# A batch-normed convolution on one Trainium2 core: one weight sum moved from GpSimd to VectorE, and one weight load split into eight transfers

## The chip, the core and the metric

The kernel runs on one core of a Trainium2 chip. The metric is the device time of one execution in microseconds (us). Engines are named as the profile names them: PE is TensorE (PEld its weight load), DVE is VectorE, ACT is ScalarE, POOL is GpSimd and SP is SyncE, which here only issues transfers. PSUM is the memory in which PE leaves its sums; it has eight banks here.

## The reference: what is computed

```python
B, S, C = 2, 2048, 1024          # x: (B, S, C), w: (3, C, C), all bfloat16
xp = jnp.pad(x, ((0, 0), (1, 1), (0, 0)))
y = sum(jnp.einsum('bsc,cd->bsd', xp[:, k:k + S, :], w[k]) for k in range(3))
inv_std = 1.0 / jnp.sqrt(var + 1e-5)
y = (y - mean) * (g * inv_std) + b
return silu(y)
```

It is a convolution of width 3 along the sequence, from 1024 to 1024 channels, with a scale and a shift for each output channel and silu behind it.

## The kernel before

**The method.** The convolution is computed in a transformed domain: six neighbouring outputs come from eight products instead of eighteen. The input is transformed once by small matmuls with a constant matrix (line 231), whose results are copied out of PSUM to `T_sb` (lines 249 and 251). The three taps of the weights become eight: tap 0 and tap 2 as they are (points j = 0 and j = 7), and three pairs (j = 1 to 6) made from a sum of taps 0 and 2, the "even sum" `e0`, `e1`, `e2` (w0 + w2, w0 + 4 w2, 4 w0 + w2), plus and minus tap 1 (for the first pair) or twice tap 1 (for the other two). The pairs are called `u`; line 150 makes each half of a pair by one instruction on POOL.

**The work.** Output channels are cut into eight blocks of 128 (`dc`), the batch has two entries (`bi`); a unit is one block for one entry, and there are sixteen, in the order (0,0), (0,1), (1,0), (1,1) and so on. A product is eight matmuls of 128x128 by 342 columns over the eight channel tiles, for one point j (line 279). A unit uses four banks, and units alternate between banks 0 to 3 and 4 to 7. Between the products ACT copies banks out (lines 288 and 290) and DVE combines them (line 294); in the end ACT applies silu (line 298) and SP stores (line 371).

**The order of PE** is written out by hand. The first unit is mixed with the input transforms (`ORDER`). In `run`, a unit's products are (bank, j) = (3,1), (0,3), (3,2), (0,4), (2,5), (2,6), with `early` (only the second unit) moving (2,5) ahead of (0,4). The last two products of a unit, j = 0 and j = 7, come during the unit behind it: `rest` gives them, and the list `also` says behind which step (`behind(1)` to `behind(6)`) they and other pieces are issued. For the second unit they are issued in the third unit, j = 0 behind step 4 and j = 7 behind step 5 (line 578). They add to banks that DVE has combined before: j = 0 to the unit's bank 0, which the combine of line 361 writes, and j = 7 to bank 3, which that of line 363 writes.

**The weights of the second block** (dc = 1) are prepared by the four pieces of `prepare_second` (line 183): the first pair on POOL; then the sum of the second (ACT scales tap 2 by 4, POOL adds); then ACT doubles tap 1 and POOL makes the second pair; and last `fourth`: ACT scales tap 0 by 4 (line 127), POOL adds tap 2 (line 137), POOL makes the third pair (line 150). `third` is issued behind step 1 of the second unit and `fourth` behind step 4 (line 576). Later blocks use `even_vector` (line 139) for their second and third sum: one DVE instruction that multiplies and adds (line 143).

**The loads** are issued by SP in the order of lines 522 to 537: input tiles `xw` of the first entry with the weights of block 0 between them, then the first two halves of the second entry, `xl` (the 48 rows left over at the end of the second entry, in three transfers of 15, 26 and 7 rows, line 534), seven more tiles, and the weights of block 1 as one transfer of 128 rows of 6 KB (line 537). A tile of the second entry reuses the place of a tile that PE has read.

Of the kernel before, what the change touches and what calls it, by code (L numbers as in the profile page):

```python
# [13 lines left out]
P = 128  # L14
# [4 lines left out]
LROWS = 48  # L19
SROW = 66  # L20
# [16 lines left out]
def kernel(  # L37
# [9 lines left out]
    nc = tc.nc  # L47
# [40 lines left out]
    xt, raw = {}, {}  # L88


    small = xlpool.tile([P, CT * P], BF16, name="xl")
    nc.vector.memset(small, 0.0)

    def load_small(bi, cuts=()):
        cuts = (0, *cuts, LROWS)
        for lo, hi in zip(cuts, cuts[1:]):
            nc.sync.dma_start(out=small[bi * SROW + lo:bi * SROW + hi], in_=xl[bi, lo:hi])

    def load_x(bi, ct, parts=1, second=nc.scalar):
        t = xpool.tile([P, NF, P], BF16, name="xw")  # L100
        xt[bi, ct] = t
        step = NF // parts
        for q in range(parts):
            s = slice(q * step, (q + 1) * step)
            (second if q else nc.sync).dma_start(out=t[:, s], in_=x[bi, ct, :, s])

    def load_w(dc, taps):
        if dc not in raw:
            raw[dc] = wpools[dc // 2 % 2].tile([P, 3, CT, P], BF16, name=f"wch{dc // 2 % 2}")
        if len(taps) == 3:  # L110
            nc.sync.dma_start(out=raw[dc], in_=w[dc])
        else:
            for k in taps:
                nc.sync.dma_start(out=raw[dc][:, k], in_=w[dc, :, k])
# [5 lines left out]
    def idle(work):  # L120
        if work:
            work.pop(0)()

    def scaled(src, by, eng):
        t = spool.tile([P, CT, P], BF16, name="w1x2")
        if eng is nc.scalar:
            nc.scalar.mul(t, src, by)
        else:
            eng.tensor_scalar(t, src, by, 0.0, op0=ALU.mult, op1=ALU.add)
        return t  # L130

    def double_w(dc, eng):
        double[dc] = scaled(raw[dc][:, 1], 2.0, eng)

    def even(dc, q, a, b):
        sums[dc, q] = epool.tile([P, CT, P], FP32, name=f"e{q}")
        nc.gpsimd.tensor_tensor(sums[dc, q], a, b, op=ALU.add)  # L137

    def even_vector(dc, q):
        w0, w2 = raw[dc][:, 0], raw[dc][:, 2]  # L140
        sums[dc, q] = e = epool.tile([P, CT, P], FP32, name=f"e{q}")
        f, h = (w2, w0) if q == 1 else (w0, w2)
        nc.vector.scalar_tensor_tensor(out=e, in0=f, scalar=4.0, in1=h, op0=ALU.mult, op1=ALU.add)  # L143

    def transform_w(dc, q, signs=(0, 1)):
        o = double[dc] if q else raw[dc][:, 1]
        if (dc, q) not in wts:
            wts[dc, q] = upool.tile([P, 2, CT, P], BF16, name=f"u{q}")
        for i in signs:
            nc.gpsimd.tensor_tensor(wts[dc, q][:, i], sums[dc, q], o, op=(ALU.add, ALU.subtract)[i])  # L150
# [32 lines left out]
    def prepare_second(dc):  # L183
        w0, w2 = raw[dc][:, 0], raw[dc][:, 2]

        def first():
            even(dc, 0, w0, w2)
            transform_w(dc, 0)

        def second():  # L190
            even(dc, 1, scaled(w2, 4.0, nc.scalar), w0)

        def third():
            double_w(dc, nc.scalar)
            transform_w(dc, 1)

        def fourth():
            even(dc, 2, scaled(w0, 4.0, nc.scalar), w2)
            transform_w(dc, 2)

        return first, second, third, fourth
# [321 lines left out]
    load_x(0, 1, 2)  # L523
    nc.sync.dma_start(out=prm, in_=prm_in)
    load_small(0)
    scales()
    nc.scalar.activation(dummy[:, 1:2], dummy[:, 0:1], ACT.Silu)
    for ct in range(2, CT):
        load_x(0, ct)
        if ct == 2:  # L530
            load_w(0, (0, 2))
    load_w(0, (1,))
    load_x(1, 0, 2, nc.sync)
    load_small(1, (15, 41))
    for ct in range(1, CT):
        load_x(1, ct)
    load_w(1, (0, 1, 2))

# [3 lines left out]
    second = list(prepare_second(1))  # L544
# [27 lines left out]
    for i, (dc, bi) in enumerate(seq[1:-1], 1):  # L572
        unit = Unit(dc, bi, i % 2 * 4)
        also = prev.rest(quiet)
        if i == 1:
            also = [(1, second[0]), (4, second[1])] + also
        if i == 2:
            also = prev.rest(quiet, 5, 4)
        if i == 3:
            also = also + [(1, lambda: idle(act_work)), (1, lambda: idle(dve_work))]  # L580
        if i == len(seq) - 2:
            also = prev.rest(quiet, 4, 5)
        unit.run(
            quiet, also,
            2 if i == 2 else dc + 2 if bi == 1 and 0 < dc < DC - 2 else None, i == 2, i == 1, i == 3,
        )
        if bi == 0 and dc + 3 < DC:
            load_w(dc + 3, (0, 1, 2))
        prev.store(nc.sync)
        prev = unit  # L590

    dc, bi = seq[-1]
# [80 lines left out]
```

## Time and profile before

| | us |
|---|---|
| three runs | 181.49, 181.79, 181.71 |
| median | 181.71 |
| the profiled execution | 181.6 |
| its span, first to last instruction | 179.8 |
| PE busy in the span | 173.3 |
| DVE busy | 148.2 |
| POOL busy | 140.6 |
| ACT busy | 110.8 |

The times of all rows of the profile are microseconds from the start of the span. A line of a timeline gives start, length, engine, line of the kernel, operation, what is written and read, and how many instructions were merged (x2); in brackets is the idle time ahead of it and what ended that. A line of the waits gives who waited for whom, the sum, how many times, and the longest. The chain that ended last is PE for 88% of the span. The clock granted to PE was 0.999 of full speed.

### The profile page before, as it was taken

To read this page: it belongs to the slowest core of one execution; us is meant where nothing else is said; L and a number is where in the kernel's file an instruction comes from. 1 tells how busy PE (TensorE), PEld (TensorE's weight loads), DVE (VectorE), ACT (ScalarE), POOL (GpSimd) and SP (SyncE) were. 2 spreads that over 40 slices of the span, in tenths; PEclk is the share of its full clock that TensorE was granted. 3 is DMA by queue.
4 is the path that set the end of the run, shared out by engine and by line. 5 is a ranking of instruction groups with operands and counts; after the bars stand their busy time and mean duration, and the time that the engine had idled before them with its cause. 6 is when DMAs were issued, how large, how long until landed. Compare 5 with 4: busy or idle time off the path is not lost.

```text
span 179.8 us, 3491 instructions
## 1 busy us (share of the span) xinstructions
PE 173.3 (96%) x1372; PEld 124.4 (69%) x1372; DVE 148.2 (82%) x193; ACT 110.8 (62%) x175; POOL 140.6 (78%) x77
## 2 busy tenths in 40 slices
PE   7889999999999999999999999999999999999991
PEld 5768888766666666666666666666666666668891
DVE  1568788987969999998898989898998997766792
ACT  3779989968364747365545654555456454573774
POOL 2499999999997979999999999999979978000000
PEclk9999999999999999999999999999999999999999
DMA  5999993170325030823073306430303020213033
GB/s 161 373 415 380 401 417 132 51 303 4 131 79 231 0 131 0 225 86 131 0 177 133 131 0 127 183 131 2 128 7 131 0 112 25 87 44 128 8 142 121
DMA packets 7507, 24.58 MB, mean 137 GB/s; under 512 B 1123, under 2 KB 1635, under 8 KB 7491
## 3 DMA queue, kind: packets, MB, share of 16 engines
q1 hardware_dynamic: 6915, 23.74, 36.1%
q10 hardware_dynamic: 576, 0.63, 1.0%
q8 instruction: 10, 0.16, 0.4%
q14 instruction: 6, 0.05, 0.1%
HBM read 14.93 MB, written 9.44 MB: 136 GB/s over the span
## 4 chain that ended last, share of the span: by engine, by line
PE 88%; DMA 5%; DVE 3%; ACT 1%; issue 0%; ACTq 0%; DVEq 0%
PE ps L279 75%; PE ps L231 8%; DMA xw<-in_x_dram 5%; PE ps L398 5%; DVE ps L294 2%; DVE t L294 1%; ACT yh L298 1%; ACT T_sb L249 1%; ACTq L78 0%; DVEq L662 0%; DVE sd L294 0%; PE ps L240 0%; PE ps L596 0%; DVEq L294 0%
## 5 line engine op out<-in xcount | busy, mean ns | idle before, releaser
L279 PE MATMUL ps<-T_sb,u 128*128 128x342 bf16 (+2 forms) x768 | 109.4, 298 | 0.0
L279 PEld LDWEIGHTS <-u 128*128 128x128 bf16 x768 | 72.2, 97 | 32.8 <-POOL u L150 0.3
L150 POOL TENSOR_TENSOR u<-e,w1x 128x1024 bf16<-128x1024 f32 x32 | 71.5, 2259 | 5.6 <-DVE e L143 5.5
L279 PE MATMUL ps<-T_sb,wch 128*128 128x342 bf16 (+2 forms) x256 | 39.5, 299 | 0.4 <-DVE ps L294 0.4
L294 DVE SCALAR_TENSOR_TENSOR t<-ps,sd 128x684 f32<-128x684 f32 (+2 forms) x49 | 37.6, 819 | 0.6
L298 ACT ACTIVATE yT<-ps,beta,scale 128x342 bf16<-128x342 f32 (+1 forms) x42 | 29.1, 727 | 12.6 <-PE ps L279 12.6
L150 POOL TENSOR_TENSOR u<-e,wch 128x1024 bf16<-128x1024 f32 x16 | 35.7, 2247 | 0.5
L279 PEld LDWEIGHTS <-wch 128*128 128x128 bf16 x256 | 24.2, 97 | 11.1 <-issue 0.5
L288 ACT COPY pc<-ps 128x342 f32<-128x342 f32 (+2 forms) x32 | 13.6, 424 | 28.4 <-PE ps L279 25.7
L249 ACT CAST T_sb<-ps 128x1008 bf16<-128x1008 f32 (+1 forms) x32 | 27.3, 879 | 3.9 <-PE ps L231 3.5
L251 DVE CAST T_sb<-ps 128x1008 bf16<-128x1008 f32 (+2 forms) x18 | 19.3, 1094 | 9.7 <-PE ps L231 9.2
L294 DVE SCALAR_TENSOR_TENSOR ps<-ps,t 128x684 f32<-128x684 f32 (+2 forms) x32 | 26.5, 829 | 0.7
L294 DVE SCALAR_TENSOR_TENSOR ps<-ps,pc 128x342 f32<-128x342 f32 (+2 forms) x34 | 16.9, 497 | 12.1 <-PE ps L279 8.8
L231 PE MATMUL ps<-rm,xw 128*128 128x168 bf16 x256 | 23.4, 239 | 1.6 <-DMA xw<-in_x_dram 1.4
L143 DVE SCALAR_TENSOR_TENSOR e<-wch 128x1024 f32<-128x1024 bf16 x12 | 24.6, 2052 | 0.0
L231 PEld LDWEIGHTS <-xw 128*128 128x128 bf16 x256 | 19.9, 99 | 4.8 <-DMA xw<-in_x_dram 2.4
L137 POOL TENSOR_TENSOR e<-wch 128x1024 f32<-128x1024 bf16 x8 | 19.0, 2372 | 0.1
L298 ACT ACTIVATE yT<-t,beta,scale 128x684 bf16<-128x684 f32 x15 | 14.4, 958 | 0.0
L294 DVE SCALAR_TENSOR_TENSOR t<-ps,t 128x684 f32<-128x684 f32 (+2 forms) x17 | 13.9, 817 | 0.0
L288 ACT COPY sd<-ps 128x342 f32<-128x342 f32 (+2 forms) x16 | 6.8, 426 | 10.3 <-PE ps L279 9.3
L290 ACT ACTIVATE pc<-ps 128x342 f32<-128x342 f32 (+2 forms) x16 | 7.0, 438 | 8.8 <-PE ps L279 6.1
L294 DVE SCALAR_TENSOR_TENSOR sd<-pc,ps 128x342 f32<-128x342 f32 (+2 forms) x17 | 8.2, 484 | 4.1 <-ACT sd L288 4.0
(45 smaller groups left out, 67.3 us busy)
## 6 DMA issues: line engine op xcount, KB each, us to landing
out_dram<-yT SPq DMA_DIRECT2D x15, 576.0 KB, 2.8
xw<-in_x_dram SPq DMA_DIRECT2D x13, 512.0 KB, 6.4
wch<-in_w_dram SPq DMA_DIRECT2D x7, 768.0 KB, 5.5
xw<-in_x_dram SPq DMA_DIRECT2D x4, 256.0 KB, 8.4
wch<-in_w_dram SPq DMA_DIRECT2D x3, 256.0 KB, 5.2
xw<-in_x_dram ACTq DMA_DIRECT2D x2, 256.0 KB, 4.6
out_dram<-yh SPq DMA_DIRECT2D x1, 256.0 KB, 2.0
out_dram<-yh SPq DMA_DIRECT2D x1, 128.0 KB
```

The costliest lines, as they stand in the source:

```text
L137: nc.gpsimd.tensor_tensor(sums[dc, q], a, b, op=ALU.add)
L143: nc.vector.scalar_tensor_tensor(out=e, in0=f, scalar=4.0, in1=h, op0=ALU.mult, op1=ALU.add)
L150: nc.gpsimd.tensor_tensor(wts[dc, q][:, i], sums[dc, q], o, op=(ALU.add, ALU.subtract)[i])
L231: nc.tensor.matmul(src[:, q // per, q % per], lhsT=xt[bi, ct][:, f + q], rhs=rm, start=True, stop=True)
L249: nc.scalar.copy(dst, src)
L251: nc.vector.tensor_copy(dst, src)
L279: nc.tensor.matmul(self.bank[q], lhsT=lhsT, rhs=T_sb[self.bi][:, ct, j, nsl], start=not add and ct == 0, stop=ct == CT - 1, skip_group_che ...
L288: nc.scalar.copy(dst, self.bank[q])
L290: nc.scalar.mul(dst, self.bank[q], by)
L294: nc.vector.scalar_tensor_tensor(out=out, in0=in0, scalar=scalar, in1=in1, op0=ALU.mult, op1=op1)
L298: nc.scalar.activation(self.yT[:, rows, self.y0:self.y0 + self.hi - self.lo], src, ACT.Silu, bias=beta[:, dc:dc + 1], scale=scale[:, dc:dc ...
L398: nc.tensor.matmul(self.bank[q], lhsT=lhsT, rhs=T_sb[self.bi][:, ct, j, :], start=not add and ct == 0, stop=ct == CT - 1, skip_group_check ...
```

## The change

The even sum of the second block's third pair is made by DVE (`even_vector`), in one instruction from the loaded taps, instead of by ACT and POOL. The piece `fourth`, with the two POOL instructions of the pair, is issued behind step 3 of the second unit instead of step 4; there it stands behind the combine of line 341 and ahead of that of line 348. The left-over rows of the second entry come in one transfer instead of three, and the weights of block 1 in eight, of 96, 1, 2, 3, 4, 5, 6 and 11 rows, instead of one. `load_w` and `load_small` change accordingly. PE's order stays as it is.

```diff
-    def load_small(bi, cuts=()):
-        cuts = (0, *cuts, LROWS)
-        for lo, hi in zip(cuts, cuts[1:]):
-            nc.sync.dma_start(out=small[bi * SROW + lo:bi * SROW + hi], in_=xl[bi, lo:hi])
+    def load_small(bi):
+        nc.sync.dma_start(out=small[bi * SROW:bi * SROW + LROWS], in_=xl[bi])
...
-    def load_w(dc, taps):
+    def load_w(dc, taps, cuts=()):
         if dc not in raw:
             raw[dc] = wpools[dc // 2 % 2].tile([P, 3, CT, P], BF16, name=f"wch{dc // 2 % 2}")
         if len(taps) == 3:
-            nc.sync.dma_start(out=raw[dc], in_=w[dc])
+            cuts = (0, *cuts, P)
+            for lo, hi in zip(cuts, cuts[1:]):
+                nc.sync.dma_start(out=raw[dc][lo:hi], in_=w[dc, lo:hi])
...
         def fourth():
-            even(dc, 2, scaled(w0, 4.0, nc.scalar), w2)
+            even_vector(dc, 2)
             transform_w(dc, 2)
...
-    load_small(1, (15, 41))
+    load_small(1)
     for ct in range(1, CT):
         load_x(1, ct)
-    load_w(1, (0, 1, 2))
+    load_w(1, (0, 1, 2), (96, 97, 99, 102, 106, 111, 117))
...
         if i == 1:
-            also = [(1, second[0]), (4, second[1])] + also
+            also = [(1, second[0]), (3, second[1])] + also
```

## The prediction

> **What bounds the kernel now.** I began with the page's busy shares, then the list of waits, then the timelines of TensorE (PE), GpSimd (POOL) and VectorE (DVE) one by one around the second and third unit, and last SyncE's queue. The page:
>
> ```profile
> PE 173.3 (96%) x1372; PEld 124.4 (69%) x1372; DVE 148.2 (82%) x193; ACT 110.8 (62%) x175; POOL 140.6 (78%) x77
> ```
>
> PE is the bound. Its matmuls follow each other without a gap from 14.2 us to 171 us, apart from one place; the first 10.8 us are the wait for the first inputs, the last 9 us are the drain of the last half unit. So the change is worth what it does to PE's gaps, and the waits have two rows for PE in its main stretch:
>
> ```profile
> PE ps L279 <- DVE ps L294: 0.4, 1, 0.4
> PEld L279 <- POOL u L150: 0.3, 1, 0.3
> ```
>
> The first is at 175.99, in the drain, which the change does not reach. The second is the place that it does reach. PE's and its weight loader's timelines:
>
> ```profile
> 47.79 1.32 PE L279 MATMUL ps<-T_sb,wch 128*128 128x342 bf16 x8
> 49.09 1.34 PE L279 MATMUL ps<-T_sb,u 128*128 128x342 bf16 x8
> ...
> 49.09 0.99 PEld L279 LDWEIGHTS <-u 128*128 128x128 bf16 x8 [0.33 <-POOL u L150]
> ```
>
> Matmuls of this shape start every 0.145 us, so eight from 47.79 would end with a start at 48.95; the next group starts at 49.09. PE loses 0.15 us there, waiting for the first product of the second block's third pair of transformed weights (u). POOL's timeline shows why:
>
> ```profile
> 40.51 4.24 POOL L150 TENSOR_TENSOR u<-e,w1x 128x1024 bf16<-128x1024 f32 x2
> 44.69 2.14 POOL L137 TENSOR_TENSOR e<-w1x,wch 128x1024 f32<-128x1024 bf16 x1
> 46.91 4.23 POOL L150 TENSOR_TENSOR u<-e,w1x 128x1024 bf16<-128x1024 f32 x2
> ```
>
> The row at 44.69 is the even sum that the change moves. POOL is busy without a gap up to 57.5, so taking 2.14 us from it brings the next pair forward.
>
> **The change, part by part.** (1) Gone: that sum on POOL, and on ScalarE (ACT) the scaling at 41.36 (1.06 us). ACT is not late for anyone here, and its three activations up to 44.96 come a microsecond earlier; its next copy (44.87) waits for PE anyway by 44.5. Value 0 for PE.
>
> (2) New on DVE: one sum of 128x1024, behind the second unit's first sd combine (40.50) and ahead of the combine at 42.18:
>
> ```profile
> 40.50 0.50 DVE L294 SCALAR_TENSOR_TENSOR sd<-pc,ps 128x342 f32<-128x342 f32 x1
> 42.18 0.52 DVE L294 SCALAR_TENSOR_TENSOR ps<-ps,pc 128x342 f32<-128x342 f32 x1 [1.18 <-PE ps L279]
> 42.74 2.42 DVE L294 SCALAR_TENSOR_TENSOR t<-ps,sd 128x684 f32<-128x684 f32 x3
> 45.08 0.51 DVE L294 SCALAR_TENSOR_TENSOR ps<-ps,pc 128x342 f32<-128x342 f32 x1
> 45.63 0.88 DVE L294 SCALAR_TENSOR_TENSOR ps<-ps,t 128x684 f32<-128x684 f32 x1
> ```
>
> There are 1.18 us of idle time. The same sum elsewhere takes 1.21 us when POOL is idle (at 147.47), but when POOL is in a sum it takes more. DVE's and POOL's rows of two such places:
>
> ```profile
> 55.76 2.83 DVE L143 SCALAR_TENSOR_TENSOR e<-wch 128x1024 f32<-128x1024 bf16 x1
> 66.87 2.64 DVE L143 SCALAR_TENSOR_TENSOR e<-wch 128x1024 f32<-128x1024 bf16 x1
> ...
> 53.29 4.21 POOL L150 TENSOR_TENSOR u<-e,wch 128x1024 bf16<-128x1024 f32 x2
> 64.21 4.22 POOL L150 TENSOR_TENSOR u<-e,w1x 128x1024 bf16<-128x1024 f32 x2 [1.22 <-DVE e L143]
> 68.38 3.12 POOL L137 TENSOR_TENSOR e<-wch 128x1024 f32<-128x1024 bf16 x1
> ```
>
> The first sum ends at 58.59, POOL's instruction at 57.50; the second at 69.51, POOL's at 68.43. Both end 1.08 us after the POOL instruction that was running when they began, and the POOL instruction behind takes 3.12 instead of 2.13. So the sum stands until POOL is through, and then POOL stands. Here DVE is free at 41.00; POOL's running transform is 40.51 to 42.64. The sum ends at 42.64 + 1.08 = 43.72. The waits for the eight transfers (step 4) lie ahead of it on DVE's queue, some 0.1 us for two of them in the trace at 53.4, thus 0.4 us: hidden, as they end near 41 and the sum stands until 42.6.
>
> An instruction behind such a sum starts 0.07 us before its end (58.51 for 58.59), so the combine of 42.18 starts at 43.65, 1.47 late, and all behind it as well: the combine of 45.63 (both inner rows, which also fixes the bank that PE adds to next) runs 47.10 to 47.98 instead of 45.63 to 46.51. The eight matmuls at 47.79 add to that bank and wait for it. With 0.06 us from DVE's end to PE's start (175.93 to 175.99 in the drain) they start at 48.03: **PE loses 0.24 us** in a new place. ACT's copy to sd at 46.87 waits for the third t (45.16, now 46.63): 0.24 to spare. DVE's lateness dies in its idle 1.50 us before 52.86: its last t there ends at 52.83 instead of 51.36.
>
> (3) On POOL the transform that begins at 42.60 takes 3.1 and ends at 45.71 (PE needs it at 46.6), and the third pair runs 45.67 to 47.80 and to 49.90. PE asks at 48.95 or, with the new loss, 49.19. **The 0.15 us go.** Later sums and pairs come 1.2 us earlier or with PE; PE waited for none of them, and the tightest slack behind (0.73 us from DVE's end at 66.96 to PE at 67.69) grows.
>
> (4) Loads. SyncE's queue:
>
> ```profile
> 10.84 2.79 SPq L97 DMA_DIRECT2D xl<-in_xl_dram  x3
> 14.68 7.84 SPq L105 DMA_DIRECT2D xw<-in_x_dram  x7
> 22.58 12.26 SPq L111 DMA_DIRECT2D wch<-in_w_dram  x3
> ```
>
> Two issues fewer at 10.84, seven more at 22.58, at 0.33 to 0.43 us each. Issues reuse eight completion counters in turn: an issue waits for the transfer eight before it. With three xl pieces, the first x tile behind waited until 14.6; with one it can go near 12.1. That gains nothing: landings of 512 KB come every 1.28 us from 19.7 to 27.4, so the transfer engines are full and order is kept. The xl data is needed at 22.88 and came at 19.7.
>
> The eight pieces of the weights: the first goes at 22.6; the last four wait for the last x tiles (24.5, 25.8, 27.1, 28.4, the landings in the trace). Before, this load was complete at 30.32, and POOL, busy until 31.97, took it at 31.92. Cost of a small transfer, from the xl pieces of 15, 26 and 7 rows: their last landings are 19.28, 19.49, 19.71, so 0.22 us each. The 96-row piece ends about 6/8 of 1.80 us (the old load's last stretch on the same engine, 28.36 to 30.16) behind 28.36, at 29.7. Seven small ones: 29.7 + 7 x 0.22 = 31.2. Lower bound 30.3 as before; upper bound 0.36 us a piece, 32.2: a 2 KB row on one engine is 0.08 us of these 0.22 (an x tile is eight 4 KB rows per engine in 1.28), so 0.14 is overhead, and a 6 KB row is 0.226 (1.80 / 8). I take 31.2, 0.7 us inside POOL's 31.92, since the xl pieces are the nearest rows: cost 0. If that cover is gone, each microsecond behind 31.92 delays POOL's chain, the sum, and PE at 48.03 one for one.
>
> In the trace the 15-row piece raises its counter by one at its issue and by 15 as data lands: 15 engines. The Trainium skill ("DMA: Bandwidth & Descriptors", section "Why a DMA increments its semaphore by 16 and not by 1") says that a transfer uses the largest number up to 16 that divides its rows, on the lowest-numbered engines; the pieces of 1, 2, 3, 4, 5, 6 and 11 rows would then all put a row on the first engine, 13 rows there against 8 before, which speaks against this split. By it I estimate 29.7 + 7 x 0.226 = 31.3, the same answer.
>
> SyncE's next issue waits for PE until 34.04, so 1.8 us more of issues cost nothing there.
>
> **Sum.** +0.24 - 0.15 = +0.09 us on the profiled execution of 181.6 (span 179.8 and 1.8 around it). The median of the runs is 181.71: **181.8 us**.
>
> **Rivals.** A, the sum above: 181.8 (chance 0.60). B, the sum does not stand, as it would if POOL's first transform came later or DVE ran through: 1.21 us from 41.0, DVE on time, only the 0.15 us gained: 181.55 (0.15). For it: the row at 147.47. Against it: that one has no POOL work beside it, and every other that begins inside a POOL instruction ends 1.08 behind one. C, slower: the weights land late. Two engines of the old load were 0.9 and 1.1 us behind the rest (30.16 and 30.32 against 29.22); if such an engine also carries the small pieces, the landing is 31.2 + 1.1 = 32.3 to 33. It decides from 31.92 on; price 0.4 to 1.1 and the 0.09: 182.2 to 182.9, middle 182.5 (0.17). For it: the last piece cannot even be issued before 28.4. Against: 0.7 us of cover. D, the sum misses the end of the transform at 42.64 and stands until 44.75: it ends at 45.83, PE loses 2.35 instead of 0.24, 183.9 (0.04). E, no effect: the stall gone is a stall regained, 181.7, cannot be told from A (0.04).
>
> **How the numbers follow.** 0.2% is 0.36 us, about what a measurement of this kernel can tell from no change; the three runs spread over 0.30. A, B and E lie within it, less their tails (0.06 to the fast side, mostly B; 0.03 to the slow side). C and D lie above, but for a little of C. Faster 0.06, same 0.71, slower 0.23. The range takes in B with its spread and most of C: 181.4 to 182.5.
>
> **What would show it.** In the profile after: the sum on DVE near 41.0 lasting about 2.75, the POOL transform behind it 3.1; the wait of the weight loader on POOL gone from 49.1; a new gap of 0.24 in PE ahead of the matmuls near 48.0, put down to DVE; POOL's first sum of the second block still at 31.92. C is right if that row starts later. A is wrong if the sum takes 1.2 (B), or if PE has gaps elsewhere between 14 and 47 us.

## The result and the profile after

| | before | changed |
|---|---|---|
| median of ten executions | 181.73 us (181.49 to 182.01) | 182.50 us (182.09 to 183.58) |
| the profiled execution | 181.6 | 182.99 |
| its span | 179.8 | 180.4 |

The ratio of the times is 1.0047, with an interval from 1.0027 to 1.0068: the changed kernel is slower, by more than the 0.2% that the prediction set as its border, and its median lies at the upper end of the predicted range. A second series of twelve executions of the same changed kernel (`g4_changed_again` below) gave 1.0033 (1.0005 to 1.0061). One execution of `f2_loads_counters_back` (184.38 us) and one of the kernel before in the last series below (184.24 us) were slow ones; they are counted in the medians and not in the ratios.

The page's first lines for the changed kernel, busy time by engine:

```profile
span 180.4 us, 3500 instructions
...
PE 173.8 (96%) x1372; PEld 124.6 (69%) x1372; DVE 149.7 (83%) x194; ACT 110.2 (61%) x174; POOL 138.6 (77%) x76
```

One instruction has gone from POOL and one from ACT, and DVE has one more. PE is still the bound, so the gaps of PE are again the question. DVE's and POOL's timelines around the moved sum:

```profile
41.21 2.85 DVE L143 SCALAR_TENSOR_TENSOR e<-wch 128x1024 f32<-128x1024 bf16 x1
43.97 0.51 DVE L294 SCALAR_TENSOR_TENSOR ps<-ps,pc 128x342 f32<-128x342 f32 x1
...
47.41 0.88 DVE L294 SCALAR_TENSOR_TENSOR ps<-ps,t 128x684 f32<-128x684 f32 x1
...
40.84 9.39 POOL L150 TENSOR_TENSOR u<-e,w1x 128x1024 bf16<-128x1024 f32 x4
```

The sum stands from 41.21 to 44.05, as forecast: it takes 2.85 us, and the combines behind it come late. POOL's four transforms are merged in one row; the first of them ends at 42.97 in the trace, 1.08 before the sum does, and the second takes 3.12. PE's timeline:

```profile
46.34 1.90 PE L279 MATMUL ps<-T_sb,u 128*128 128x342 bf16 x12
48.34 1.32 PE L279 MATMUL ps<-T_sb,wch 128*128 128x342 bf16 x8
49.49 1.33 PE L279 MATMUL ps<-T_sb,u 128*128 128x342 bf16 x8
```

Twelve starts at 0.145 us from 46.34 put the last at 47.93; the next start is 48.34, 0.41 later, so 0.26 us are lost there. From 48.34 to 49.49 are eight starts without a loss: the 0.15 us of before, at 49.09, have gone.

So far this is the predicted +0.1. What was not forecast lies elsewhere. First, SyncE's waits in the last four microseconds, of the kernel before and then of the changed one (total, number, longest):

```profile
SPq L662 <- DMA out_dram<-yh: 1.5, 4, 0.6
```

```profile
SPq L662 <- DMA out_dram<-yh: 1.7, 1, 1.7
```

At the end of the program SyncE waits for the completion counters in a fixed order, by five instructions one behind the other. Before, four of these waits end by a landing in turn. After, the first of them waits 1.7 us for the last store alone, and the others follow it. The trace gives the starts of the last ones: before 178.94 and 179.00, after 179.35, 179.41, 179.47, 179.54 and 179.60. Each costs 0.063 us. Before, the last store stood on the counter that the fourth instruction waits for, so one more followed its landing; with the change it stands on a counter of the first instruction, and four follow. From the last matmul's start to the end of the span it was 3.44 us before and is 3.66 after: **0.2 us**.

Secondly, the weights. They were complete at 30.32 before, and are at 32.04 now. POOL's first sum of the second block in its timeline with the row ahead of it, before and then after, and of SyncE's waits after the one of the weights' issues for x tiles (total, number, longest):

```profile
27.74 4.22 POOL L150 TENSOR_TENSOR u<-e,w1x 128x1024 bf16<-128x1024 f32 x2
31.92 2.13 POOL L137 TENSOR_TENSOR e<-wch 128x1024 f32<-128x1024 bf16 x1
```

```profile
27.90 4.22 POOL L150 TENSOR_TENSOR u<-e,w1x 128x1024 bf16<-128x1024 f32 x2
32.25 2.12 POOL L137 TENSOR_TENSOR e<-wch 128x1024 f32<-128x1024 bf16 x1
```

```profile
SPq L111 <- DMA xw<-in_x_dram: 4.8, 4, 1.9
```

Before, the sum starts 0.04 us ahead of the end of POOL's earlier work (31.92 for 31.96); after, it starts at 32.25, 0.16 us later than that work (up to 32.12) would let it. It starts 0.21 us behind the landing at 32.04, and in the five other profiles below in which POOL was late it follows the landing by 0.20 or 0.21 us as well (for instance 32.10 for 31.89 in `g4`). To be in time, the weights thus had to land by about 31.71 and not by 31.92. Four of the eight issues stood for 4.8 us behind x tiles, the last of them until 29.88.

Thirdly, what lies outside the span was 1.8 us in the profiled execution of before and 2.59 in that of after. There the trace has a fetch of instructions (16 KB, 0.88 us) at 182.36, behind the last instruction.

In this profile PE was also 0.3 us later than before by 31 us: the first matmuls behind the inputs came 0.14 later, and at 18.68 it lost 0.13. Neither is put down to the change: `e1_sum_alone` below, with the old loads, began 0.13 later, and `e4_before_counters_on`, with the old loads too, lost as much at 18.46. One small loss does go with the left-over rows in one transfer: the x tile behind them was issued over 2 us earlier and yet landed at 20.84 to 21.17 in the kernels with one transfer and at 20.46 to 20.86 in those with three (without `e2` and `f3`, which began late). In five of the eight profiles with one transfer (`e3`, `f1`, `g1`, `g3`, `g4`) PE loses 0.04 to 0.09 us near 21 us, where it waits for this tile, and in none of the six with three.

### The profile page after: what moved, and what is told of

Same layout as the page of the kernel before. It is cut to its first block, busy times and chain, and to the rows that moved or that the text cites. A ratio compares the mean times of both kernels' runs of the same rounds, so it can differ in the third digit from the quotient of the medians.

```text
span 180.4 us, 3500 instructions
## 1 busy us (share of the span) xinstructions
PE 173.8 (96%) x1372; PEld 124.6 (69%) x1372; DVE 149.7 (83%) x194; ACT 110.2 (61%) x174; POOL 138.6 (77%) x76
## 4 chain that ended last, share of the span: by engine, by line
PE 82%; DVE 8%; DMA 5%; ACT 1%; issue 1%; DVEq 0%; ACTq 0%
PE ps L279 69%; PE ps L231 8%; DMA xw<-in_x_dram 5%; PE ps L398 5%; DVE ps L294 3%; DVE t L294 2%; DVE e L143 2%; DVE f L294 1%; ACT yh L298 1%; ACT T_sb L249 1%; ACTq L78 0%; DVE sd L294 0%; DVEq L662 0%; PE ps L240 0%; DVEq L143 0%
## 5 line engine op out<-in xcount | busy, mean ns | idle before, releaser
L150 POOL TENSOR_TENSOR u<-e,w1x 128x1024 bf16<-128x1024 f32 x32 | 70.4, 2223 | 7.7 <-DVE e L143 5.2
L150 POOL TENSOR_TENSOR u<-e,wch 128x1024 bf16<-128x1024 f32 x16 | 36.7, 2314 | 0.5
L143 DVE SCALAR_TENSOR_TENSOR e<-wch 128x1024 f32<-128x1024 bf16 x13 | 26.6, 2043 | 0.0
```

## The experiments

All were timed in five rounds, in three series; each series has its own executions of the kernel before, with medians of 181.88 (35 executions), 181.89 (35) and 181.87 (29). The medians of its span were 180.0, 179.9 and 179.9. The ratio, with its interval, is an estimate of its own from these executions and not the quotient of the two medians. "Tail" is the time from the last matmul's start to the end of the span, in the profiled execution; "late" is how much later POOL's first sum of the second block started for its weights there (0.04 more than the idle time of its row, by the overlap named above).

| kernel | median, us (executions) | ratio to before | median span | tail | late |
|---|---|---|---|---|---|
| e1_sum_alone | 181.82 (12) | 0.9997 (0.9982 to 1.0012) | 180.0 | 3.44 | 0 |
| e2_loads_alone | 182.58 (12) | 1.0045 (1.0024 to 1.0066) | 180.6 | 3.63 | 0.14 |
| e3_after_counters_back | 182.13 (12) | 1.0021 (0.9995 to 1.0048) | 180.3 | 3.45 | 0.50 |
| e4_before_counters_on | 182.00 (12) | 1.0000 (0.9976 to 1.0023) | 180.1 | 3.63 | 0 |
| f1_equal_pieces | 182.54 (12) | 1.0033 (1.0005 to 1.0061) | 180.6 | 5.18 | 0.62 |
| f2_loads_counters_back | 182.53 (12) | 1.0018 (0.9990 to 1.0045) | 180.45 | 5.02 | 0.40 |
| f3_sum_behind_5 | 181.75 (12) | 0.9985 (0.9959 to 1.0012) | 179.8 | 3.44 | 0 |
| f4_thirteen_more | 182.63 (12) | 1.0023 (0.9991 to 1.0054) | 180.1 | 3.65 | 0 |
| g1_weights_whole | 182.05 (12) | 1.0003 (0.9981 to 1.0024) | 180.1 | 3.45 | 0 |
| g2_sum_behind_5_one_more | 181.49 (12) | 0.9979 (0.9962 to 0.9996) | 179.7 | 3.38 | 0 |
| g3_weights_ahead | 183.60 (6) | 1.0094 (1.0064 to 1.0123) | 181.85 | 3.65 | 0 |
| g4_changed_again | 182.28 (12) | 1.0033 (1.0005 to 1.0061) | 180.25 | 3.64 | 0.27 |

The theory was: the sum costs what the prediction says (+0.1), and the rest comes from the loads, by two mechanisms, the counters at the end (0.2) and the late weights. The rivals: the sum costs more than the profile shows; and the weights are late because their uneven pieces crowd on one transfer engine.

Several edits need a store cut in parts, which adds transfers and so turns the counters on. The helper is the same in all of them:

```diff
-        def store(self, queue):
-            queue.dma_start(out=out[self.bi, self.dc].rearrange("p (i n) -> p i n", i=R), in_=self.yT)
+        def store(self, queue, parts=1):
+            to = out[self.bi, self.dc].rearrange("p (i n) -> p i n", i=R)
+            cuts = [R * k // parts for k in range(parts + 1)]
+            for lo, hi in zip(cuts, cuts[1:]):
+                queue.dma_start(out=to[:, lo:hi], in_=self.yT[:, lo:hi])
...
-        prev.store(nc.sync)
+        prev.store(nc.sync, 4 if i == 8 else 1)
```

### The sum alone

`e1_sum_alone` is the kernel before with the sum on DVE at step 3; its loads are the old ones.

```diff
-            even(dc, 2, scaled(w0, 4.0, nc.scalar), w2)
+            even_vector(dc, 2)
...
-            also = [(1, second[0]), (4, second[1])] + also
+            also = [(1, second[0]), (3, second[1])] + also
```

> The kernel before with the sum on VectorE alone, issued behind step 3; the loads as before. Theory (three terms: the sum, the order of the last waits, a part outside the span): the sum's own term only. TensorE waits 0.24 near 48 and no longer 0.15 near 49, so +0.1 us against before, 181.8; from TensorE's last product to the end of the span 3.8 us as before; time less span 1.8. Rival (the sum is the whole loss, by what it shifts later on VectorE and GpSimd): +0.6 to +0.8, 182.4.

Measured: 0.9997, a span of 180.0 as before. DVE's and PE's timelines of this kernel:

```profile
41.03 2.84 DVE L143 SCALAR_TENSOR_TENSOR e<-wch 128x1024 f32<-128x1024 bf16 x1
...
46.31 1.75 PE L279 MATMUL ps<-T_sb,u 128*128 128x342 bf16 x11
48.16 1.32 PE L279 MATMUL ps<-T_sb,wch 128*128 128x342 bf16 x8
49.31 1.33 PE L279 MATMUL ps<-T_sb,u 128*128 128x342 bf16 x8
```

The last of the eleven starts at 47.75 (46.31 and ten times 0.145), the next at 48.16: 0.41 again, a loss of 0.26, and no gap at 49.31. The sum does in the timeline what the prediction said, and the time doesn't move by what can be measured. The rival that the sum costs more falls: the interval ends at +0.22 us, and the rival asked for +0.6 at least. (The 3.8 us that the theory gives for the end of the span is a slip: before, it is 3.44.)

### The loads alone

`e2_loads_alone` is the kernel before with the new loads (line 534 and 537 and their two helpers as in the change) and the sum left on ACT and POOL.

```diff
-    load_small(1, (15, 41))
+    load_small(1)
...
-    load_w(1, (0, 1, 2))
+    load_w(1, (0, 1, 2), (96, 97, 99, 102, 106, 111, 117))
```

> The kernel before with the changed loads alone (the left-over rows in one transfer, the second block's weights in eight); the sum as before on GpSimd. Theory: the part outside the sum, +0.4 to +0.7, 182.1 to 182.4: 0.19 at the end because the last store's counter is then the first of the eight that SyncE waits for and four more waits of 0.06 follow, the rest between span and time in some of the executions. GpSimd's first sum of the second block starts some 0.2 late, and TensorE waits 0.3 near 49 where it waited 0.15. Rival (the sum is the loss): 181.7.

Measured: 1.0045, the whole loss of the change, with a tail of 3.63. The loss comes with the loads. (The profiled execution was 1.7 us later than before by its 300th matmul, mostly by its first inputs, so its rows around 48 us are not used.)

### The counters, turned back and turned on

`e3_after_counters_back` is the changed kernel with the eighth store cut in four, three transfers more, so that the last store gets the counter that it had before. `e4_before_counters_on` is the kernel before with the same store cut in six, five transfers more: the counters of the changed kernel at the end, with the old loads.

```diff
-        prev.store(nc.sync, 4 if i == 8 else 1)
+        prev.store(nc.sync, 6 if i == 8 else 1)
```

> The changed kernel with one store in the middle (of the eighth unit's output) cut in four, three transfers more, so that the last stores use the same completion counters as before the change. Theory: the end is 0.19 shorter, 182.3 if only the order of the last waits counts; if the part outside the span hangs on these counters too, 181.8 to 182.0. Rival (the end does not depend on the counters): 182.5.

> The kernel before with that store cut in six, five transfers more, so that the last stores use the counters that they have in the changed kernel. Theory: +0.19 at the end of the span, 181.9; if the part outside the span hangs on the counters, 182.2 to 182.4. Rival (no dependence): 181.7.

SyncE's last waits, of e3 and then of e4:

```profile
SPq L665 <- DMA out_dram<-yh: 1.5, 4, 0.6
```

```profile
SPq L665 <- DMA out_dram<-yh: 1.7, 1, 1.7
```

The two rows have changed places: the changed kernel with the counters back ends like the kernel before (tail 3.45), and the kernel before with the counters on ends like the changed one (3.63). The tail's 0.2 us are thus the place of the last store's counter among the last waits. The times go the same way: 1.0021 for e3 against 1.0033 and 1.0047 of the changed kernel, and a span of 180.1 against 180.0 for e4. But 0.2 us is 0.1%, less than half of each interval: the mechanism is shown by the trace, its effect on the median is not told from zero by the times alone.

### Equal pieces

`f1_equal_pieces` is the changed kernel with eight pieces of 16 rows.

```diff
-    load_w(1, (0, 1, 2), (96, 97, 99, 102, 106, 111, 117))
+    load_w(1, (0, 1, 2), (16, 32, 48, 64, 80, 96, 112))
```

> The changed kernel with the second block's weights in eight equal pieces of 16 rows instead of 96, 1, 2, 3, 4, 5, 6 and 11. Theory (the split's number, not its sizes, makes the loss: the last piece cannot be issued before the last input tile is in, and the counters of the last stores move): the weights complete near 31.5 instead of 32.0, GpSimd's first sum of the block at 32.0 to 32.1, span 180.3, time 182.3 to 182.5, and the end of the span as in the changed kernel. Rival (the uneven rows make it, by loading the first engine with 13 rows): landing below 30.5, span 180.1 or less, time below 182.0.

The weights were complete at 32.33, not earlier than with the uneven pieces (32.04 and 31.89), and later than the theory's 31.5 too. The uneven rows are not what makes them late; what the two have in common is eight pieces, the last of them issued at 29.98 here and at 29.88 there. The time is not better either (1.0033), but this kernel has something else: in its profiled execution a fetch of instructions began at 178.21, the last store landed late, and the tail is 5.18.

It also has a surprise on DVE. POOL came 0.62 late, and then the sum began just ahead of POOL's transform; DVE's row and POOL's:

```profile
41.00 1.22 DVE L143 SCALAR_TENSOR_TENSOR e<-wch 128x1024 f32<-128x1024 bf16 x1
...
41.14 9.35 POOL L150 TENSOR_TENSOR u<-e,w1x 128x1024 bf16<-128x1024 f32 x4
```

It took 1.22 us, PE had no gap near 48 or 49, and its last matmul started at 176.30, earlier than before (176.37). That is the prediction's rival B, come about by the lateness of rival C: being later is not always worse for this sum.

### The loads with the counters back

`f2_loads_counters_back` is `e2_loads_alone` with the eighth store cut in four.

> The kernel before with the changed loads alone and one middle store cut in four, so that the last stores use the counters that they had before the change; the sum stays on GpSimd. Theory: the end of the span is as before (3.44 from the last matmul), what is left is the late landing of the weights, near 32, which delays GpSimd's chain by 0.2 to 0.3 and TensorE by as much near 49: span 180.2 to 180.4, time 182.1. Rival (late landing is free, the loss of the loads is all in the counters): span 180.0, time 181.8.

The ratio is 1.0018 (0.9990 to 1.0045) for 1.0045 of e2, but the two intervals overlap, and again a fetch of instructions (at 178.43) lay in the tail (5.02) of the profiled execution. So the times don't tell how much the counters were. What its profile does show is the price of late weights with the sum left on POOL. POOL's and PE's rows:

```profile
32.36 2.13 POOL L137 TENSOR_TENSOR e<-wch 128x1024 f32<-128x1024 bf16 x1 [0.36 <-DMA wch<-in_w_dram]
...
48.09 1.32 PE L279 MATMUL ps<-T_sb,wch 128*128 128x342 bf16 x8
49.55 1.34 PE L279 MATMUL ps<-T_sb,u 128*128 128x342 bf16 x8
```

Eight starts from 48.09 end at 49.11; the next is at 49.55, 0.44 later: PE loses 0.29 us at POOL's pair instead of 0.15. That is 0.14 us more, in an execution in which PE itself was 0.3 us later than before by its 300th matmul.

### The sum one step further on

`f3_sum_behind_5` is the kernel before with the sum on DVE behind step 5.

```diff
-            also = [(1, second[0]), (4, second[1])] + also
+            also = [(1, second[0]), (5, second[1])] + also
```

> The kernel before with the sum on VectorE, but two steps later (behind step 5), after the three t combines of the second unit and before the combine of the two middle banks; the loads as before. Theory: GpSimd is idle then, so the sum takes 1.2 us, from 45.1 to 46.3; the pair of GpSimd starts near 46.4 and its first half is there at 48.5; the combine that TensorE waits for ends 1.2 later, at 47.7, just in time; neither the 0.24 near 48 nor the 0.15 near 49 remains: span 0.1 below the kernel before, time 181.7 to 181.75 beside 181.85 of before. Rival (VectorE's end is late again): a gap of 0.1 to 0.2 near 48, no gain.

The sum came at 46.65 (the profiled execution was 1.6 us later than before by its 300th matmul), when POOL had run out of work and waited for it, and took 1.22 us; PE had no gap at 48 or 49. The ratio is 0.9985, and 1 lies in its interval (0.9959 to 1.0012): a gain is not shown.

### Thirteen transfers more

`f4_thirteen_more` is the kernel before with three stores cut in five, six and five: the same place on the counters as five more, by other transfers (it was to tell the number of transfers from their place).

```diff
-        prev.store(nc.sync, 4 if i == 8 else 1)
+        prev.store(nc.sync, {6: 5, 8: 6, 10: 5}.get(i, 1))
```

> The kernel before with three middle stores cut in 5, 6 and 5, thirteen transfers more: the last stores use the same counters as in the changed kernel, with eight transfers more than there. Theory: the end of the span is 0.19 longer, and the executions with over 2 us between span and time are as frequent (4 to 6 of 12) as in the three kernels with those counters so far (15 of 34; 10 of 59 in the others). Rival (chance, or the number of transfers): 2 of 12, and time 181.9.

The tail is 3.65 and the span 180.1, both as in e4. The median is higher, 182.63, because six of twelve executions had over 2 us outside the span, for four in e4. That is as many as the theory forecast, but the kernel before, beside it, had 15 of 35. The span goes by the place on the counters; that what lies outside it does so too is not shown.

### The weights whole

`g1_weights_whole` is the changed kernel with the weights of block 1 in one transfer again and the eighth store cut in three, which brings the counters back as well.

```diff
-    load_w(1, (0, 1, 2), (96, 97, 99, 102, 106, 111, 117))
+    load_w(1, (0, 1, 2))
...
-        prev.store(nc.sync, 4 if i == 8 else 1)
+        prev.store(nc.sync, 3 if i == 8 else 1)
```

> The changed kernel with the second block's weights in one transfer again, and one middle store cut in three, so that the last stores use the counters that they had before the change; the sum on VectorE and the left-over rows in one transfer stay. Theory (the sum is worth +0.1 or less, the rest comes from the eight pieces: their late landing and the counters): as the kernel with the sum alone, span 180.0, time 181.8 beside 181.9 of before. Rival (the single transfer of the left-over rows does harm): as the changed kernel less 0.2, 182.2.

The weights were complete at 30.82, POOL wasn't late, the tail was 3.45 (PE was 0.4 us later than before by 31 us, so its profile has no gap near 48 and is not used for that), and the ratio is 1.0003 (0.9981 to 1.0024). With the sum on DVE and the left-over rows in one transfer, but neither late weights nor turned counters, no loss can be told from zero; one of up to 0.24% lies in the interval. Between this kernel and e3, which have the same tail, stand the eight pieces (and one part more of the cut store): 180.3 against 180.1 in the median span, where the kernels before of the two series had 180.0 and 179.9.

### The sum behind step 5, and one transfer more

`g2_sum_behind_5_one_more` is `f3_sum_behind_5` with the eighth store cut in two, which puts the last store on the counter that is waited for last.

> The kernel before with the sum on VectorE behind step 5, and one middle store cut in two, so that the last store's counter is among the last two that SyncE waits for. Theory: the sum there takes 0.15 off TensorE's span and the order of the waits another 0.06: tail 3.38, span 179.75, time 0.15 to 0.2 below before. Rival (the order of the waits is worth nothing): as with the sum behind step 5 alone, 0.1 below before.

DVE's, POOL's and PE's rows of this kernel:

```profile
45.28 1.22 DVE L143 SCALAR_TENSOR_TENSOR e<-wch 128x1024 f32<-128x1024 bf16 x1
...
46.58 4.22 POOL L150 TENSOR_TENSOR u<-e,w1x 128x1024 bf16<-128x1024 f32 x2 [1.59 <-DVE e L143]
...
46.25 1.90 PE L279 MATMUL ps<-T_sb,u 128*128 128x342 bf16 x12
47.99 1.32 PE L279 MATMUL ps<-T_sb,wch 128*128 128x342 bf16 x8
49.15 1.33 PE L279 MATMUL ps<-T_sb,u 128*128 128x342 bf16 x8
```

PE's starts follow each other through both places, the tail is 3.38, the shortest of all, and the median 181.49 us: 0.9979 (0.9962 to 0.9996). POOL stands idle for 1.59 us ahead of its third pair and nobody waits for that. It is the one kernel here whose interval lies below 1. Its median is 0.38 us below that of the kernel before, of which the two terms of the theory explain 0.21; it also had over 2 us outside the span in only one execution of twelve, the kernel before in nine of 29, which no run puts down to the edit.

### The weights ahead of two tiles

`g3_weights_ahead` is the changed kernel with the eight pieces issued ahead of the last two x tiles, so that they land early; it was to give the price of the lateness.

```diff
     for ct in range(1, CT):
+        if ct == CT - 2:
+            load_w(1, (0, 1, 2), (96, 97, 99, 102, 106, 111, 117))
         load_x(1, ct)
-    load_w(1, (0, 1, 2), (96, 97, 99, 102, 106, 111, 117))
```

> The changed kernel with the eight transfers of the second block's weights issued ahead of the last two input tiles instead of behind them; their sizes, their number and the counters at the end stay. Theory (the late landing costs 0.1 to 0.3): the weights are in by 30, GpSimd starts its first sum of the block without a wait near 31.9, span 180.1 to 180.2, the end 0.2 longer than before as in the changed kernel, time 0.2 below the changed kernel of the same call. Rival (late landing is free): same as the changed kernel.

This missed. POOL was on time (32.01), but the two x tiles, which were issued behind the pieces at 29.21 and 29.67 only, landed at 32.56 and 33.84, and PE waited for the first of them; the row of PE:

```profile
32.60 0.61 PE L231 MATMUL ps<-rm,xw 128*128 128x168 bf16 x6 [2.04 <-DMA xw<-in_x_dram]
```

The ratio is 1.0094, and the run says nothing on the price of late weights.

### The changed kernel again

> The changed kernel itself, beside the other three on one chip. Both theories: 182.3 to 182.6, span 180.3 to 180.4; its share of executions that fetch a block of instructions near or behind the end (over 0.7 above its fastest) tells whether the 6 of 10 of the first series was chance: the theory says 3 to 7 of 12, as in the kernels with the changed loads so far (22 of 46 over their fastest by 0.7), beside 19 of 70 for the kernel before.

In this execution PE's 300th matmul starts at 31.07, for 31.02 before (it began 0.09 earlier behind its inputs and lost 0.10 near 18.7 and 20.9), so the losses behind it can be read off. POOL's row and PE's:

```profile
32.10 2.13 POOL L137 TENSOR_TENSOR e<-wch 128x1024 f32<-128x1024 bf16 x1 [0.21 <-POOL u L150]
...
46.24 1.75 PE L279 MATMUL ps<-T_sb,u 128*128 128x342 bf16 x11
48.19 1.32 PE L279 MATMUL ps<-T_sb,wch 128*128 128x342 bf16 x8 [0.19 <-DVE ps L294]
```

The last of the eleven starts at 47.69, and the next at 48.19: 0.50 for 0.145, a loss of 0.355. That is the 0.26 of e1 and 0.1 more, as POOL was late by its weights and the sum on DVE stands until POOL is through. The row puts POOL's idle time down to its own earlier instruction; by the trace the weights were complete at 31.89, and the sum starts 0.21 us behind that, as in the other kernels with late weights.

The last matmul starts at 176.60, for 176.37 before: +0.23, of which 0.21 is 0.355 less the 0.147 gone at 49. The tail is 3.64, for 3.44: +0.20. Together 0.43 of the 0.44 between the two spans (180.25 and 179.81). Four of the twelve executions were over 0.7 us above the fastest, which fits the theory's 3 to 7 but also the 8 of 29 of the kernel before, so it tells nothing.

## Why the prediction was wrong

**Part by part.** (1) Right: ACT and POOL each lost an instruction, and PE waited for neither. (2) Right in place, mechanism and size: the sum stood until 1.08 us behind the end of POOL's instruction, and PE lost 0.26 near 48 for a forecast of 0.24 (e1). (3) Right: the 0.15 at POOL's pair went in e1 and in the changed kernel.

(4) is the step that failed: that the loads cost nothing ("I take 31.2, 0.7 us inside POOL's 31.92, since the xl pieces are the nearest rows: cost 0"). Two things were wrong in it.

- The weights landed at 32.04 and 31.89 instead of 31.2, and POOL, which needed them by about 31.71 and not by 31.92, lost 0.16 and 0.27. The prediction let the last piece go at 28.4, when the x tile that it waits for landed before. That tile itself landed at 29.87: in the trace its last seven packets of 4 KB start 0.27 us apart, where they were 0.16 apart before. It is the pieces that do this, as g1, with the weights whole and else the same loads, landed this tile at 28.80; that those already under way shared the engines with it is the likely way. The x tiles came 1.28 us apart down to 26.17, and then 1.49 and 2.20 (in g4 1.81 and 1.84). The last piece was issued at 29.88 and ended two microseconds later. So the transfers added behind a queue slowed the very transfer that the last of them waited for. The first piece, of 96 rows, was not done at 29.7 either, but at 31.83 and 30.91 (g4): the 6 KB packets of the weights took 0.38 and 0.34 us at the median, for 0.23 before. The upper bound of the working, 32.2, held both landings; the value taken for the sum did not.
- The eight completion counters were used in the working only for the waits of issues in the load phase. They run on through the whole kernel. With five transfers more, every later transfer stands five counters on, and the last store comes on one that is waited for early, with four waits of 0.063 us behind it instead of one: 0.2 us (e3, e4 and f4 turn it on and off). No part of the prediction looked at the end of the program.

That the left-over rows in one transfer gain nothing was right, but they may also cost a little: the 0.04 to 0.09 us near 21 us named above, for which no run gives a price in the time.

The median of the first ten lies on the upper end of the range. That is no merit of the working: this end came from rival C, whose price was wrong, and some 0.3 us of that median lie outside the span, for which the prediction had no term.

**The rivals.** C had the right place and the wrong price: weights behind 31.92 delay POOL, the sum and PE, but by 0.1 in g4, not by the 0.4 to 1.1 that the prediction set. It asked for a late engine's 1.1 us on top of 31.2; the lateness came from the last issue instead, and the prediction had even put that issue down as what spoke for C. Equal pieces landed no earlier (f1), so the crowding on the first engine was not the cause. That crowding was worked out by the rule of the Trainium skill ("DMA: Bandwidth & Descriptors", section "Why a DMA increments its semaphore by 16 and not by 1"), and the estimate of 31.3 by it took the same early issue. B did not come in the changed kernel, but a sum that does not stand did in f1, and behind step 5 in f3 and g2. D did not come. E was wrong by the loads, not by the sum.

**The sum of it.** In spans, of the profile that compares best (g4): 0.26 - 0.15 for the sum, 0.1 for late weights, 0.2 for the counters, 0.4 in all (the 0.10 lost ahead of 31 us was made up by inputs that came 0.09 earlier). That is what the second series measured between the medians (182.28 and 181.87).

**What stays open.** The first series gave 0.77 between the medians, 0.3 more. Its six executions of ten with over 2 us outside the span make most of that (its median span of 180.4 and the usual 1.8 would be 182.2); in the second series of the same kernel it was five of twelve, and in the three series of the kernel before 32 of 99 together. Where such an execution was profiled (the changed kernel twice, e2), a fetch of instructions of about a microsecond began 1.0 to 2.0 us behind the end of the span. All kernels with the changed kernel's counters at the end had 28 of 76, all with those of before 47 of 159: whether the change makes such executions more frequent, the counts don't tell. Another count does differ: a span of 181.0 us or more came in 16 of 70 executions of the kernels with the weights in eight pieces behind the tiles (the changed kernel in its two series, e2, e3, f1 and f2), and in 7 of 171 of those with one transfer. No run was made to explain it. Of those that were profiled, f1 and f2 have a fetch among the last stores, and e2 and f3 late first inputs, and the first ten of the changed kernel have none, so it is not the 0.3. The price of late weights on the median rests on one gap in one profile and on the spans of e3 and g1; g3, which was to measure it, did not.

## What to carry to other kernels

Completion counters that are used in turn make the number of transfers a property of the whole program: a load cut in pieces changes what every later issue waits for and how many waits follow the last store, so the end of the trace is to be read for a change at the start. When a transfer is cut and queued behind others, the time at which its last piece may be issued has to be taken with the new pieces already in the engines, not from the landings of before. And an operation that stands while another engine is at work is best put where that engine has to wait for it anyway: behind step 5 the same sum took 1.22 us instead of 2.85, and PE had no gap there.

## What the runs showed of the hardware

Who begins first decides what the sum of line 143 takes: 2.84 to 2.93 us when it began inside a transform of POOL (41.21, 41.03 and 40.97 in the changed kernel, e1 and g4), 2.42 when it began later inside one (41.31 in g1), and 1.22 when it began 0.14 us ahead of POOL's (f1). Whenever it began inside, it ended 1.08 us behind the transform's end. The Trainium skill ("SBUF — State Buffer", section "🔬 SBUF: two separate sides") says that VectorE, with two inputs in SBUF, and GpSimd share a pair of ports as an exclusive lock, which whoever starts first holds for its whole instruction. These rows agree with it, and they add that the sum got its turn at the border between two POOL instructions that followed each other, and that the second then took 3.12.

The fetches of instructions of 16 KB took 0.9 to 2.0 us in these traces, most of them about 1.0. In f1 and f2, where one began at 178.2 and 178.4, among the last stores, the tail was 1.5 us longer (5.18 and 5.02 for 3.6 and 3.45); where one began behind the last instruction (the changed kernel twice, e2 and g2), the time outside the span was 1.9 to 2.9 us instead of 1.8. A fetch of 1.0 us at 15.63 also goes with the late engine that rival C leaned on: in the kernel before, the sixteen counts of each of the three transfers that landed from 14.62 to 16.53 came within 0.6 us, and from the next x tile on the last count of each came 0.8 to 1.1 us behind the other fifteen. A second fetch, at 26.90, goes with the second late count of the old load (30.16 and 30.32 for 29.22).
